# Layer two's second half: its second product in seven products too, and the leads set anew

## The chip, the cores and the metric

The kernel runs on one core of a Trainium2 chip. The core has five engines that each run their own instruction list: PE (TensorE, matmuls, with its weight loads listed as PEld), DVE (VectorE), ACT (ScalarE), POOL (GpSimd) and SP (SyncE), which here only issues DMAs. They meet through semaphores. The metric is the device time of one execution in microseconds.

## The reference

Attention of 8 heads over 4 x 576 positions (half of the heads see the last 32 positions, half every 32nd), then two feed-forward layers on 2304 tokens of 512 features, all in float32:

```python
# layer one (hidden size 1536): xn = x / rms(x) * rms_g
y = (silu(xn @ w_gate) * (xn @ w_val)) @ w_out
# layer two (hidden size 2048)
h = y @ w_in
out = (np.maximum(h, 0.0) ** 2) @ w_out
```

## The kernel before

**Precision.** Every factor of a product is split in two parts of float32r, hi = round(v) (ACT or DVE) and lo = v - hi (DVE or POOL). A product of a 128 x 128 block is then three matmuls: hi x hi, hi x lo, lo x hi. I call a factor that is split so a *form*.

**Stages.** Phase 0 is the first half of layer one and is interleaved with the attention. Phase 1 is the rest of layer one (three pairs of 128 hidden features, `j`), phases 2 and 3 are the two halves of layer two's hidden features (four pairs each). In phases 1 to 3 the tokens go in three pairs `q` of two tiles of 384 (`n` = 0, 1).

**The seven-product form.** The first product of each layer (x times `w_in`) in phases 1 to 3 is a 2 x 2 block product (two token tiles, two hidden blocks, two halves of the 512 features), done with seven block products instead of eight: sums and differences of the x blocks and of the weight blocks are made beforehand, and the seven results P1, P5, P6, P2, P7, P3, P4, in this order, are added up. `product` (L1785) issues six matmuls for each at L1806: two feature blocks of 128 x three. PSUM bank A takes P1; once it is copied out as s1, P6 and P7 and P4 are added on to A by PE. D takes P5 and then P3. C takes P2, which DVE adds to s1 (L1841). ReLU and square follow (L1857, L1905 to L1908), and the hidden tile is split (L1934 hi, L1941 lo).

**The second product**, hidden times `w_out`, is done plainly in all phases: `a_step` (L1955) takes one hidden tile of 128 features and one token tile and issues 4 output blocks x 3 matmuls (`mm3`, L1361 to L1363) into four banks that are accumulated over all `j`. In phase 3 the results of phase 2 (kept in `yq_d`) are added when the banks are read (L2010).

**x blocks.** For each `q` of phases 1 to 3, `pair_task` loads x (L1618), makes four differences (L1650) and seven forms (L1657, L1659 hi, L1664 lo) of 768 columns in `ra`. Phases 2 and 3 both do this, from the same data.

**Weights** come as raw float64 words (`wst_a<-in_w`), are converted on DVE and POOL, split, stored to DRAM (`wi_d` for the first product, `wo_d` for the second), and loaded again (L1344).

**What sets the order.** PE's order is a fixed list. All else (which engine takes an operation that two could do, and where in its list it stands) is decided while the kernel is built, by a planner that keeps a clock for each engine, takes the task that can start first, and breaks near ties by due times. Due times are positions in the stages less a lead (`W2_LEAD`, `X2_LEAD`, `PREP_LEAD` and others). Filler matmuls (`fill`, L2155) are put in where the planner sees PE waiting in the beginning.

Of the kernel before, what the change touches and what calls it, by code (L numbers as in the profile page):

```python
# [56 lines left out]
ATT_LEAD, ATT_STEP = 6.5, 0.25  # L57
PREP_LEAD = 4.192
W_LEAD = 0.5
X_LEAD = 2.784  # L60
# [4 lines left out]
TOL = 0.144  # L65
# [8 lines left out]
NM2 = 10  # L74
# [3 lines left out]
PRI = {"qk": -3, "mask": 4, "mx": 2, "exp": 1, "eps": 2, "sum": 8, "norm": -3, "turn": 1, "keep": 20, "tr": -1,  # L78
       "swap": -1, "pv": 3, "out": 0, "sq": -3, "ms0": 2, "add": 0}
MXP, LOADF, BIAS = 10, 0.5, 0.729  # L80

D_BUSY, D_COST, D_LATE, D_COST2 = 111.519, 1.1, 250.0, 0.5
PV_AHEAD = 4
# [20 lines left out]
NHID = len(HID_AT)  # L104
PRODUCTS = [
    ("P1", 0, 0, "A", None), ("P5", 3, 1, "D", None), ("P6", 4, 2, "A", "s1"), ("P2", 1, 3, "C", None),
    ("P7", 5, 4, "A", "u2"), ("P3", 6, 5, "D", "s5"), ("P4", 2, 6, "A", "c22"),
]
W2_LEAD, X2_LEAD, L2_LEAD = 3.0, 2.9, 3.0
X2_PRI = 1.0  # L110
# [90 lines left out]
def kernel(ctx: ExitStack, tc: tile.TileContext, loc, strd, w1, w2, g, cst, out):  # L201
# [73 lines left out]
    wo_d = {(ph, j): dram.tile([128, 2, 2, 512], F32R, name=f"wo_d{ph}{j}") for ph in NJS for j in range(NJS[ph])}  # L275
# [838 lines left out]

    def through(cell, t):
        cell["n"] += 1
        if cell["n"] == 2:
            cell["t"] = t

    def w_task(n, due):  # L1120
# [11 lines left out]
        def size(parts, t):  # L1132
            if not two:
                cell["w"], cell["ring"] = ring_take(n)
            if two:
                o = 1024 * is_out((ph2, j2, m2))
# [83 lines left out]
    def raw_ready(n):  # L1220
        k = n - U1
        return latest(done.get("raw"), *(done.get(("w2",) + u) for u in units2[:k] if not is_out(u) or is_out(units2[k])))

    def sums_ready(ph, j, m):
        k = units2.index((ph, j, m))
        return latest(0.0, *(done.get(("w2",) + u) for u in units2[:k] if is_out(u)))
# [34 lines left out]
    def pieces(ph, j, m):  # L1261

        outer = is_out((ph, j, m))

# [25 lines left out]
        def lo(a, b, o, c):  # L1290
            w = b - a

            def store(t):
                src = stage(c["n"])[:, 0:2 * w].bitcast(F32).rearrange("p (h c) -> p h c", h=2)
                if outer:
                    dst = wo_d[ph, j][:, o // 512]
                else:
                    dst = wi_d[ph, j, m][:, :, o:o + w]
                nc.sync.dma_start(out=dst.bitcast(F32), in_=src)
                end = lanes.dma(2 * w, t)  # L1300
                stage_t[c["n"]] = end
                if b == 2048:
                    done["stored", ph, j, m] = end

            def f(parts, t):
# [3 lines left out]
                if b == 2048:  # L1309
                    done["w2", ph, j, m] = t  # L1310
                spawn([Task(-2000, [(None, [[("Q", 0.0)]], lambda _, t: store(t), None)])], t)
# [3 lines left out]
        if not outer:  # L1315
# [281 lines left out]

    def pair_task(ph, q, due):
# [44 lines left out]
        def block(b, r, add, after):  # L1643
# [17 lines left out]
            def lo(parts, t):  # L1661
# [4 lines left out]
                done["xb", ph, q, b] = t  # L1666
                cell["n"] += 1
# [107 lines left out]
    def bank_take():  # L1775
        b = min((b for b in banks if bank_time(b) is not None), key=bank_time)
# [7 lines left out]

    def product(ph, q, j, m, p):  # L1785
        name, a, b, role, need = PRODUCTS[p]
        key = ph, q, j, m
# [36 lines left out]
    def after_product(key, name, c, at_t):  # L1824
# [12 lines left out]

        def add(what, role, h, n):
# [15 lines left out]
        def relu(h, n):  # L1854
            def f(_, t):
                e = f_take(ph)
                nc.scalar.activation(  # L1857
                    out=e["ap"](), in_=c["A"]["ap"][:, :SN], func=ACTF.Silu if ph == 1 else ACTF.Relu
                )
                c["A"]["t"] = t  # L1860
# [5 lines left out]
            if ph == 1 and m:  # L1866
                times_gate(None, h, n, at_t)
# [10 lines left out]
        def times_gate(e, h, n, at_t):  # L1878

            def f(_, t):  # L1880
                x = gates.pop((q, j, h, n))
                v = c["A"]["ap"][:, :SN] if e is None else e["ap"]()
                o = e or x
                nc.vector.tensor_tensor(out=o["ap"](), in0=v, in1=x["ap"](), op=ALU.mult)
                if e is None:
                    c["A"]["t"] = t
# [11 lines left out]
        def square(e, h, n, clipped, at_t):  # L1898
            seq = h_seq[ph, q, n, j, h]

            def f(parts, t):
# [7 lines left out]
                spawn([split(seq, e, -1000 + at[key] if n == 0 else -1000 + at[ph, q, "t"])], t)  # L1909
# [6 lines left out]
            "P1": lambda: copy("s1", "A"), "P5": lambda: copy("s5", "D"), "P6": lambda: copy("u2", "A"),  # L1916
            "P2": lambda: add("s1", "C", 0, 0), "P7": lambda: add("s5", "A", 1, 1), "P3": lambda: add("u2", "D", 0, 1),
            "P4": lambda: relu(1, 0),
# [11 lines left out]
    def split(seq, e, due):  # L1930
# [7 lines left out]
        def lo(parts, t):  # L1938
# [4 lines left out]
            e["t"] = t  # L1943

# [10 lines left out]
    def a_step(ph, q, n, j, h):  # L1955
# [7 lines left out]
        def f(ms):  # L1963
            def g(_, t):
                if first:
                    acc2[key] = [bank_take() for _ in range(KDM)]
                x, w = hid2(seq), w_out(j)[:, h]
# [10 lines left out]
        tail = ph == 3 and q == NQ - 1 and n == 1 and last  # L1978
        parts = [range(m, m + 1) for m in range(KDM)] if tail else [range(KDM)]
        return [(lambda: times() is not None, mms(SN, 3 * len(parts[0])), f(parts[0]), times)] + [  # L1980
            (None, mms(SN, 3), f(p), None) for p in parts[1:]
        ]
# [4 lines left out]
    def after_a(ph, q, n, ms, at_t):  # L1987
        cell = outs.setdefault((ph, q, n), {"n": 0, "t": 0.0, "ys": False})
        t0 = 2 * SN * q + SN * n
        dst = y1_d[:, :, t0:t0 + SN] if ph == 1 else (  # L1990
            yq_d[q][n] if ph == 2 else out[:, t0:t0 + SN].rearrange("(m p) t -> p m t", p=128)
        )
        tail = ph == 3 and q == NQ - 1 and n == 1
# [5 lines left out]

        def store_part(m):  # L2000
            return lambda t: nc.sync.dma_start(out=dst[:, m], in_=ys2[:, m])

        def evict(m):
            def f(parts, t):
# [4 lines left out]
                if ph != 2:  # L2009
# [8 lines left out]
                if tail:  # L2018
                    transfer(-2000, t, SN, store_part(m))
                if cell["n"] == KDM:  # L2020
                    if ph != 2:
                        done["yp2", ph, 2 * q + n] = cell["t"]
                    if not tail:
                        transfer(-2000, cell["t"], KDM * SN, store)
# [5 lines left out]
        def when():  # L2030
            return max(0.0 if cell["ys"] else rel["ys"][0], done["ypt", ph, q, n] if ph != 2 else 0.0)
# [4 lines left out]
    def yp2_task(ph, q, n, due):  # L2036
        nth = 2 * q + n

        def when():
            t0 = 2 * SN * q + SN * n  # L2040
            stored = [
                ("yp", i) for i, (o, m) in enumerate(BLOCKS) if o < t0 + SN and o + m > t0
            ] if ph == 1 else [("yq", 2, q, n)]
            if nth:
                before = [done.get(("yp2", ph, nth - 1))]
            elif ph == 1:
                before = [done.get("late")]
            else:
                before = [done.get(("in_used", 2, NJS[2] - 1))] + [f_time(e, 2) for e in f_tiles if e["last"] == 2]
            return latest(*before, *map(done.get, stored))  # L2050

        def load(_, t):
            if ph == 3 and nth == 0:
                for e in f_tiles:
                    if e["last"] == 2:
                        e["last"] = 0
            v = late["fb"][:, 0:KDM * SN].rearrange("p (k c) -> p k c", k=KDM)
            t0 = 2 * SN * q + SN * n
            nc.sync.dma_start(out=v, in_=yp_d[:, :, t0:t0 + SN] if ph == 1 else yq_d[q][n])
# [4 lines left out]

    slots = [(0, i, j) for i in range(NB) for j in range(PHASES[0][2])]
# [3 lines left out]
    starts = {1: ((0.0, 0.9), (1.8, 2.8), (4.1, 5.1)), 2: ((0.0,), (1.0,), (2.6,), (4.2,))}  # L2069
    for ph in NJS:  # L2070
        for q in range(NQ):
            for j, os in enumerate(starts[min(ph, 2)]):
                for m, o in enumerate(os):
                    at[ph, q, j, m] = n_at + o
            at[ph, q, "t"] = n_at + (6.3 if ph == 1 else 5.8)
            n_at += 8.3 if ph == 1 else 8.7
# [20 lines left out]
    for ph in NJS:  # L2097
        for q in range(NQ):
            pair_task(ph, q, at[ph, q, 0, 0] - X2_LEAD)
            for n in range(2):  # L2100
                if ph != 2:
# [3 lines left out]
    for ph, j, m in units2:  # L2105
# [3 lines left out]
        else:  # L2109
# [9 lines left out]
    for ph in NJS:  # L2119
        nj = NJS[ph]  # L2120
        for q in range(NQ):
            for j in range(nj):
                ps = [product(ph, q, j, m, p) for m in range(MATS[ph]) for p in range(len(PRODUCTS))]
                if j:
# [8 lines left out]
            for n, js in ((0, [nj - 1]), (1, range(nj))):  # L2133
# [6 lines left out]
    with tc.manual_schedule():  # L2140
# [45 lines left out]
        while tasks:  # L2186
            if "fb" not in late and order.get("prep", 0) == NB and all(
# [4 lines left out]
                late["fb"] = pool("fb", 1).tile([128, 6144], F32, name="fb")  # L2192
                late["rb"] = pool("rb", 1, reuse_waits="tile").tile([128, 2048 * NJS[1]], F32R, name="rb")
                late["fc"] = ExitStack()
                late["fd"] = pool("fd", 1, late["fc"]).tile([128, 2048], F32, name="fd")
            if not advance():
# [77 lines left out]
```

## Time and profile before

| | us |
|---|---|
| median of 3 runs (lowest, highest) | 906.1 (905.36, 907.96) |
| profiled execution, its own time | 904.4 |
| span of the profile, first to last instruction | 902.6 |
| mean granted clock of TensorE, share of full speed | 0.996 |

In the profile, a group row reads: line, engine, operation, output<-input, shapes, count, then busy us and the mean ns of one, then the idle time of the engine just ahead of these instructions and what ended it. Matmuls are pipelined: a row's length is that from a matmul's start to its modelled end, and the next starts before that end. The stages of the profile by time: phase 0 with the attention to about 298 us, phase 1 to about 512, phase 2 to about 712, phase 3 to the end.

### The profile page before, as it was taken

To read this page: it belongs to the slowest core of one execution; us is meant where nothing else is said; L and a number is where in the kernel's file an instruction comes from. 1 tells how busy PE (TensorE), PEld (TensorE's weight loads), DVE (VectorE), ACT (ScalarE), POOL (GpSimd) and SP (SyncE) were. 2 spreads that over 40 slices of the span, in tenths; PEclk is the share of its full clock that TensorE was granted. 3 is DMA by queue.
4 is the path that set the end of the run, shared out by engine and by line. 5 is a ranking of instruction groups with operands and counts; after the bars stand their busy time and mean duration, and the time that the engine had idled before them with its cause. 6 is when DMAs were issued, how large, how long until landed. Compare 5 with 4: busy or idle time off the path is not lost.

```text
span 902.6 us, 17050 instructions
## 1 busy us (share of the span) xinstructions
PE 884.5 (98%) x6809; PEld 827.7 (92%) x6814; DVE 652.8 (72%) x1071; ACT 441.8 (49%) x1107; POOL 80.3 (9%) x69
## 2 busy tenths in 40 slices
PE   8999999899999999999999999999999999999998
PEld 5778787788788999999999999999999999999998
DVE  5999967868868666967957968768869568346433
ACT  5978737332323454454444555457355445343441
POOL 0243400101000000200101101001000000000000
PEclk9999999999999999999999999999999999999999
DMA  9766643565675999999898796552673953302203
GB/s 342 248 234 202 204 146 96 201 228 168 210 291 186 373 380 348 371 390 363 312 355 320 282 343 232 177 193 103 229 266 142 380 202 104 107 1 71 71 1 105
DMA packets 74607, 202.50 MB, mean 224 GB/s; under 512 B 6432, under 2 KB 38176, under 8 KB 69792
## 3 DMA queue, kind: packets, MB, share of 16 engines
q1 hardware_dynamic: 74528, 201.42, 62.3%
q8 instruction: 53, 0.87, 0.4%
q14 instruction: 26, 0.21, 0.1%
HBM read 136.97 MB, written 60.82 MB: 219 GB/s over the span
## 4 chain that ended last, share of the span: by engine, by line
PE 84%; DVE 7%; DMA 6%; ACT 2%; issue 1%; SPq 0%; POOL 0%; DVEq 0%
PE a L1806 16%; PE pg L1806 8%; PE a L1361 7%; PE a L1362 7%; PE a L1363 7%; PE pb L1806 5%; DMA wst_a<-in_w 5%; PE gv L1361 5%; PE gv L1362 4%; PE gv L1363 4%; PE pg L1363 2%; PE pg L1361 2%; PE pg L1362 2%; PE pb L1363 2%; PE pb L1362 2%; PE pb L1361 2%
## 5 line engine op out<-in xcount | busy, mean ns | idle before, releaser
L1806 PE MATMUL a<-ra 128*128 128x384 f32 x990 | 189.0, 335 | 1.0 <-DVE fa L1841 1.0
L1806 PEld LDWEIGHTS a<-ra 128*128 128x128 f32 x990 | 173.7, 188 | 2.0 <-DVE fa L1841 1.9
L1806 PE MATMUL pg<-ra 128*128 128x384 f32 x492 | 95.7, 335 | 1.5 <-DVE fb L1841 1.4
L1361 PE MATMUL gv<-ra 128*128 128x512 f32 (+1 forms) x240 | 91.2, 380 | 0.4 <-DVE fa L1438 0.4
L1362 PE MATMUL gv<-ra 128*128 128x512 f32 (+1 forms) x240 | 88.9, 370 | 0.0
L1363 PE MATMUL gv<-ra 128*128 128x512 f32 (+1 forms) x240 | 88.7, 370 | 0.0
L1806 PEld LDWEIGHTS pg<-ra 128*128 128x128 f32 x492 | 86.3, 188 | 2.3 <-DVE fb L1841 1.7
L1363 PE MATMUL a<-ra,rb 128*128 128x384 f32 x216 | 72.6, 336 | 0.0
L1361 PE MATMUL a<-ra,rb 128*128 128x384 f32 x216 | 72.6, 336 | 0.0
L1362 PE MATMUL a<-ra,rb 128*128 128x384 f32 x216 | 72.6, 336 | 0.0
L1664 DVE TENSOR_TENSOR ra<-fb,ra 128x768 fp32r<-128x768 f32 x63 | 59.0, 953 | 1.6 <-ACT ra L1657 0.9
L1806 PE MATMUL pb<-ra 128*128 128x384 f32 x282 | 55.7, 336 | 0.3 <-DVE ra L1664 0.3
L1361 PEld LDWEIGHTS gv<-ra 128*128 128x128 f32 x240 | 45.5, 190 | 8.4 <-DVE fa L1438 0.6
L1363 PEld LDWEIGHTS gv<-ra 128*128 128x128 f32 x240 | 45.5, 190 | 7.8
L1362 PEld LDWEIGHTS gv<-ra 128*128 128x128 f32 x240 | 45.6, 190 | 7.3 <-DVE ra L934 0.3
L1806 PEld LDWEIGHTS pb<-ra 128*128 128x128 f32 x282 | 49.5, 188 | 0.8 <-DVE ra L1664 0.6
L1657 ACT ACTIVATE ra<-fb 128x768 fp32r<-128x768 f32 x47 | 39.3, 841 | 22.1 <-DVE fb L1650 12.9
L1308 DVE TENSOR_TENSOR wst_a<-fa,wst_a 128x512 fp32r<-128x512 f32 (+1 forms) x59 | 37.4, 638 | 15.8 <-ACT wst_a L1285 15.1
L1361 PE MATMUL a<-ra 128*128 128x512 f32 (+1 forms) x120 | 45.4, 379 | 2.3 <-ACT pt L545 1.5
L1285 ACT ACTIVATE wst_a<-fa 128x512 fp32r<-128x512 f32 (+1 forms) x60 | 34.3, 577 | 26.6 <-DMA wi_d<-wst_a 14.8
L1308 POOL TENSOR_TENSOR wst_a<-fa,wst_a 128x512 fp32r<-128x512 f32 (+1 forms) x19 | 26.3, 1383 | 221.3 <-ACT wst_a L1285 199.5
L1362 PE MATMUL a<-ra 128*128 128x512 f32 (+1 forms) x120 | 44.4, 370 | 0.1
(215 smaller groups left out, 1937.7 us busy)
## 6 DMA issues: line engine op xcount, KB each, us to landing
ra<-wi_d SPq DMA_DIRECT2D x26, 1792.0 KB, 8.2
wst_a<-in_w SPq DMA_DIRECT2D x34, 1024.0 KB, 6.6
wi_d<-wst_a SPq DMA_DIRECT2D x42, 512.0 KB, 4.9
wo_d<-wst_a SPq DMA_DIRECT2D x22, 512.0 KB, 10.2
rb<-wo_d SPq DMA_DIRECT2D x9, 1024.0 KB, 6.8
fb<-y_d SPq DMA_DIRECT2D x24, 384.0 KB, 4.9
fa<-in_strd SPq DMA_DIRECT2D x8, 604.0 KB, 5.9
fa<-in_loc SPq DMA_DIRECT2D x8, 592.0 KB, 5.3
```

What stands on the lines that cost most here:

```text
L1285: nc.scalar.activation(out=dst, in_=raw(a, b), func=ACTF.Copy)
L1308: eng.tensor_tensor(out=x[:, w:2 * w], in0=raw(a, b), in1=x[:, 0:w].bitcast(F32), op=ALU.subtract)
L1361: nc.tensor.matmul(out=o, lhsT=whi, rhs=x_hi, start=first, stop=False)
L1362: nc.tensor.matmul(out=o, lhsT=whi, rhs=x_lo, start=False, stop=False)
L1363: nc.tensor.matmul(out=o, lhsT=wlo, rhs=x_hi, start=False, stop=last)
L1657: nc.scalar.activation(out=x[:, 0], in_=src, func=ACTF.Copy)
L1664: eng.tensor_tensor(out=x[:, 1], in0=src, in1=x[:, 0].bitcast(F32), op=ALU.subtract)
L1806: nc.tensor.matmul(out=o, lhsT=l, rhs=v, start=need is None and k + n == 0, stop=k == 1 and n == 2, skip_group_check=need is not None,)
```

## The change

**The second product of phase 3** takes the seven-product form too. Its 2 x 2 blocks are the two token tiles, the two hidden blocks `h` of each pair `j`, and two halves of 256 output features. For each `q` there are seven products of four steps `j`, each step six matmuls (`o_step`, two output blocks x three). The hidden tiles stay as float32 until `hidden_form` makes the seven sums, differences and forms of each `j` from them, in up to twelve places (four in `ra`, eight new ones `rx`). The weight forms are made in `pieces` and stored in seven tensors `wf_d`; `o_load_task` brings them through four buffers (`ORING`). `after_o` adds each product's result to the output tile in `wst_a`, which starts as phase 2's result, and stores it.

**x forms of phase 3** are no longer made: phase 2 stores its seven forms per `q` to `xf_d` (`keep_form`), phase 3 loads them (`form_task`).

**The seed.** In phases 1 to 3, except for the first set, P1 is copied by ACT (DVE may take it too) into bank C (`seed`), and PE adds P2 onto it; ACT then reads the finished sum (`relu` with role C) where DVE had to add P2 to s1.

**Leads and costs** are set anew. They move instructions of the attention stage and of the weight preparation.

```diff
-W2_LEAD, X2_LEAD, L2_LEAD = 3.0, 2.9, 3.0
+W2_LEAD, X2_LEAD, L2_LEAD = 5.974, 3.127, 3.0
-    ("P1", 0, 0, "A", None), ("P5", 3, 1, "D", None), ("P6", 4, 2, "A", "s1"), ("P2", 1, 3, "C", None),
+    ("P1", 0, 0, "A", None), ("P5", 3, 1, "D", None), ("P6", 4, 2, "A", "s1"), ("P2", 1, 3, "C", "s1"),
+O_ORDER = [(0, 0), (0, 1), (1, 0), (1, 1), (0, 2), (1, 2), (0, 3), (1, 3)]
+O_ORDER += [(p, j) for p in range(2, 7) for j in range(4)]
...
+        def seed(what, role, to):
+            def f(parts, t):
+                c[to] = bank_take(True)
+                o, i = c[to]["ap"][:, :SN], c[role]["ap"][:, :SN]
+                if parts[0][0] == "A":
+                    nc.scalar.activation(out=o, in_=i, func=ACTF.Copy)
+                else:
+                    nc.vector.tensor_copy(o, i)
+                c[what] = t
...
-            "P1": lambda: copy("s1", "A"), "P5": lambda: copy("s5", "D"), "P6": lambda: copy("u2", "A"),
-            "P2": lambda: add("s1", "C", 0, 0), "P7": lambda: add("s5", "A", 1, 1), "P3": lambda: add("u2", "D", 0, 1),
+            "P1": lambda: seed("s1", "A", "C") if seeded(ph, q, j) else copy("s1", "A"), ...
+            "P2": lambda: relu("C", 0, 0) if seeded(ph, q, j) else add("s1", "C", 0, 0), ...
...
+        def load(_, t):
+            nc.sync.dma_start(out=x_slot2(b).bitcast(F32), in_=xf_d[q, b].bitcast(F32))
...
+    PARTS = [
+        ((0, 0), None, ()), ((0, 0), ((0, 1), (0, 0)), (("lo", 0),)), ((0, 0), ((1, 1), (0, 0)), (("lo", 1),)),
+        ((1, 0), None, ()), ((0, 1), ((1, 1), (0, 1)), (("sum", 1),)), ((1, 1), None, ()),
+        ((1, 0), ((1, 0), (0, 0)), (("lo", 3), ("sum", 2))),
+    ]
+    def hidden_form(q, j, p, seq, due):
...
+        def total(parts, t):
+            eng = nc.gpsimd if parts[0][0] == "P" else nc.vector
+            eng.tensor_tensor(out=tile_of(dst), in0=tile_of(add[0]), in1=tile_of(add[1]), op=ALU.subtract)
...
+        def lo(parts, t):
+            eng = nc.gpsimd if parts[0][0] == "P" else nc.vector
+            x = halves()
+            eng.tensor_tensor(out=x[:, 1], in0=tile_of(dst), in1=x[:, 0].bitcast(F32), op=ALU.subtract)
...
+    def o_load_task(q, p, due):
+        n = len(PRODUCTS) * q + p
+        a = PRODUCTS[p][1]
+        def when():
+            before = done.get(("out_used", 2, n)) if n < ORING else done.get(("o_used", n - ORING))
...
+    def o_step(q, p, j, ms=range(2)):
...
+            for m in ms:
+                w_hi, w_lo = (w[:, h, 128 * m:128 * m + 128] for h in range(2))
+                for i, (l, v) in enumerate(((w_hi, x[:, 0]), (w_hi, x[:, 1]), (w_lo, x[:, 0]))):
+                    nc.tensor.matmul(
+                        out=c[role, m]["ap"][:, :SN], lhsT=l, rhs=v, start=need is None and first and i == 0,
+                        stop=last and i == 2, skip_group_check=need is not None,
+                    )
...
+    def after_o(q, name, c, ms, at_t):
+        m0, n, role, what, end, frees = {
+            "P1": (0, 0, "A", "s1", False, False), "P5": (2, 1, "D", "s5", False, False),
+            "P6": (0, 1, "A", "u2", False, False), "P2": (0, 0, "C", None, True, True),
+            "P7": (2, 1, "A", "c22", True, False), "P3": (0, 1, "D", None, True, True),
+            "P4": (2, 0, "A", None, True, True),
+        }[name]
...
+                if ph == 3:
+                    row = ps
+                    if j == nj - 1:
+                        o = [o_step(q, p, i) for p, i in O_ORDER]
+                        if q == NQ - 1:
+                            o[-4:] = [o_step(q, 6, i, range(m, m + 1)) for m in range(2) for i in range(4)]
+                        row = ps[:3] + o[:2] + ps[3:5] + o[2:4] + ps[5:] + o[4:]
```

How this moves instructions, at three places. PE, the end of the program, before: the last output blocks of `a_step` for the last hidden tile (banks `a_...` and `pg_...`, hidden tile in `ra`, weights in `rc`).

```order
L1361 MATMUL a_3912<-ra,rc 128x384
L1362 MATMUL a_3912<-ra,rc 128x384
L1363 MATMUL a_3912<-ra,rc 128x384
L1361 MATMUL pg_3836<-ra,rc 128x384
L1362 MATMUL pg_3836<-ra,rc 128x384
L1363 MATMUL pg_3836<-ra,rc 128x384
```

The same place now: the last steps of P3 (forms in `rx_...`) and P4 (forms in `ra`); L2269 is `o_step`'s matmul.

```order
L2269 MATMUL a_3946<-rx_7151,rc 128x384 x3
L2269 MATMUL pg_3872<-rx_7152,rc 128x384 x3
L2269 MATMUL a_3946<-rx_7152,rc 128x384 x3
L2269 MATMUL pg_3917<-ra,rb 128x384 x12
L2269 MATMUL a_3945<-ra,rb 128x384 x12
```

Four banks that ran over all hidden tiles have become pairs of banks that run over the four `j` of one product.

ACT, the last set of first products in phase 3, before: L1832 copies P1, P5 and P6 out of PSUM, L1905 and L1906 are ReLU and square, L1934 is hi of a hidden form.

```order
L1832 ACTIVATE fa<-pg_3836 128x384
L1832 ACTIVATE fa<-a_3911 128x384
L1832 ACTIVATE wst_a<-pg_3836 128x384
L1905 ACTIVATE fa<-fa 128x384
L1906 ACTIVATE fa<-fa 128x384
L1934 ACTIVATE ra<-fa 128x384
```

The same place now: L1901 is the seed (PSUM bank to PSUM bank), L1890 copies P5 and P6 out, L1928 reads the finished sum from bank C, L1977 is the square, L2181 is hi of a hidden form.

```order
L1901 ACTIVATE pb_3836<-a_3945 128x384
L1890 ACTIVATE fa<-pg_3917 128x384
L1890 ACTIVATE wst_a<-a_3945 128x384
L1928 ACTIVATE fa<-pb_3836 128x384
L1977 ACTIVATE fa<-fa 128x384
L2181 ACTIVATE ra<-fa 128x384 x2
```

The copy of P1 now goes to a bank, and ACT reads the sum of P1 and P2 itself.

SP, phase 3 from its first output store on, before (`y_d` holds x, `yq_d` phase 2's result):

```order
L1996 DMA out<-fa 128x4x384
L2059 DMA fb<-yq_d_117 128x1536
L1618 DMA fb<-y_d 128x2x384 x4
L1996 DMA out<-fa 128x4x384
L2059 DMA fb<-yq_d_118 128x1536
```

And now, from the x forms of the second pair on: L1635 loads an x form, L2217 the weight form of one product into the ring, L2293 stores output.

```order
L1635 DMA ra<-xf_d_162 128x1536
L1635 DMA ra<-xf_d_163 128x1536
L2217 DMA rb<-wf_d_148 128x2048
L2217 DMA rb<-wf_d_149 128x2048
L2217 DMA rb<-wf_d_145 128x2048
L2217 DMA rc<-wf_d_143 128x2048
L2293 DMA out<-wst_a 128x384 x2
L2217 DMA rb<-wf_d_146 128x2048
```

The loads of the ring stand behind all x loads of the next pair, and output stores between them.

## Rows read from the trace of the kernel before

**Rows 1.** The page, part 1: busy us, share of the span, instructions.

```profile
PE 884.5 (98%) x6809; PEld 827.7 (92%) x6814; DVE 652.8 (72%) x1071; ACT 441.8 (49%) x1107; POOL 80.3 (9%) x69
```

**Rows 2.** By stage: us, busy of PE, PEld, DVE, ACT, POOL, clock, DMA share, GB/s.

```profile
0.00:298.00 298.00, 287.23 (x3354) 233.51 (x3360) 241.68 (x397) 159.26 (x573) 47.62 (x42) 0.99 0.64 215
298.00:512.00 214.00, 211.79 (x1245) 209.85 (x1244) 160.46 (x258) 101.05 (x187) 21.42 (x18) 1.00 0.92 347
512.00:712.00 200.00, 198.46 (x1140) 197.80 (x1139) 153.52 (x247) 102.60 (x194) 11.26 (x9) 1.00 0.63 225
712.00:898.00 186.00, 186.00 (x1072) 185.83 (x1071) 95.54 (x168) 78.87 (x153) 0.00 (x0) 1.00 0.28 98
```

**Rows 3.** Timeline of PE: start us, length us, line, operation.

```profile
8.99 3.88 PE L2155 MATMUL warm<-blank 128*128 128x512 bf16 x17 [0.16 <-issue]
...
58.79 0.61 PE L430 MATMUL sc<-cst_sb 128*128 128x384 f32 x2
...
876.33 0.34 PE L1363 MATMUL pg<-ra,rb 128*128 128x384 f32 x1
...
879.45 0.34 PE L1363 MATMUL pb<-ra,rc 128*128 128x384 f32 x1
```

**Rows 4.** PE's waits: us in total, times, longest.

```profile
PE xo L578 <- issue: 4.3, 2, 2.3
...
PE pg L1806 <- DVE fb L1841: 1.4, 1, 1.4
PE bc L886 <- DVE sm L456: 1.4, 1, 1.4
PE a L1806 <- DVE fa L1841: 1.0, 3, 0.4
...
PE pb L1806 <- DVE ra L1664: 0.3, 1, 0.3
PE pg L1806 <- ACT fb L1832: 0.2, 1, 0.2
```

**Rows 5.** DMA issues: count, KB each, median us to landing.

```profile
ra<-wi_d SPq DMA_DIRECT2D x26, 1792.0 KB, 8.2
...
rb<-wo_d SPq DMA_DIRECT2D x9, 1024.0 KB, 6.8
```

**Rows 6.** DVE's groups by shape, 712 to 898 us.

```profile
L1664 DVE TENSOR_TENSOR ra<-fb,ra 128x768 fp32r<-128x768 f32 x14 | 13.0, 954 | 0.5 <-ACT ra L1657 0.4
L1941 DVE TENSOR_TENSOR ra<-fa,ra 128x384 fp32r<-128x384 f32 x20 | 11.0, 554 | 4.0 <-ACT ra L1934 3.8
...
L1650 DVE TENSOR_TENSOR fb<-fb 128x768 f32<-128x768 f32 x8 | 7.6, 953 | 0.1
...
L1941 DVE TENSOR_TENSOR ra<-wst_a,ra 128x384 fp32r<-128x384 f32 x13 | 7.0, 555 | 5.9 <-ACT ra L1934 5.9
```

**Rows 7.** ACT's groups by shape, 712 to 898 us.

```profile
L1657 ACT ACTIVATE ra<-fb 128x768 fp32r<-128x768 f32 x8 | 6.7, 838 | 1.1 <-PE a L1806 0.6 <-PE pg L1806 0.6
...
L1832 ACT ACTIVATE fa<-a 128x384 f32<-128x384 f32 x10 | 4.9, 492 | 5.4 <-PE a L1806 5.3
```

**Rows 8.** Timeline of DVE at two places.

```profile
346.49 0.56 DVE L1884 TENSOR_TENSOR fa<-pg,fa 128x384 f32<-128x384 f32 x1
...
347.90 0.55 DVE L1941 TENSOR_TENSOR ra<-fa,ra 128x384 fp32r<-128x384 f32 x1
...
684.63 1.83 DVE L1664 TENSOR_TENSOR ra<-fb,ra 128x768 fp32r<-128x768 f32 x2
```

**Rows 9.** Timeline of POOL and DVE at two places.

```profile
433.44 1.33 POOL L1308 TENSOR_TENSOR wst_a<-fa,wst_a 128x512 fp32r<-128x512 f32 x1 [2.64 <-issue]
433.51 1.67 DVE L1884 TENSOR_TENSOR fd<-fd 128x384 f32<-128x384 f32 x1
...
495.63 0.91 POOL L1271 TENSOR_TENSOR fa<-fa 128x256 f32<-128x256 f32 x1 [11.15 <-DVE fa L1165]
```

**Rows 10.** Timeline of DVE, its last instruction.

```profile
899.07 0.56 DVE L2010 TENSOR_TENSOR fa<-pg,fb 128x384 f32<-128x384 f32 x1
```

More of the change, by code (lines that the diff above doesn't have):

```diff
@@ L64 @@
 DRAIN = 0.12
-TOL = 0.144
+TOL = 0.141
 FILL, FILL_OF, T0, W1_AT = 0.215, 0.85, 5.3, 11.631
@@ L1263, in pieces @@
         outer = is_out((ph, j, m))
+        forms = outer and ph == 3
         def raw(a, b):
@@ L1976, in f @@
             return g
[L1978 to L1982, printed above, removed]
+        return [(lambda: times() is not None, mms(SN, 3 * KDM), f(range(KDM)), times)]
     ys2 = qa[:, YS2:YS2 + KDM * SN].rearrange("p (k c) -> p k c", k=KDM)
@@ L1989, in after_a @@
         t0 = 2 * SN * q + SN * n
[L1990 to L1993, printed above, removed]
+        dst = y1_d[:, :, t0:t0 + SN] if ph == 1 else yq_d[q][n]
         def store(t):
@@ new lines, in o_slot, with when, load @@
+    def o_slot(n):
+        n %= ORING
+        a = late["rc"] if n == NJS[1] else late["rb"][:, 2048 * n:2048 * n + 2048]
+        return a.rearrange("p (j h c) -> p j h c", j=NJS[3], h=2)
+    def o_load_task(q, p, due):
+        n = len(PRODUCTS) * q + p
+        a = PRODUCTS[p][1]
+        def when():
+            before = done.get(("out_used", 2, n)) if n < ORING else done.get(("o_used", n - ORING))
+            return latest(before, *(done.get(("stored", 3, j, MATS[3])) for j in range(NJS[3])))
+        def load(_, t):
+            nc.sync.dma_start(out=o_slot(n).bitcast(F32), in_=wf_d[a].bitcast(F32))
+            done["o_in", n] = lanes.dma(2048, t)
+        tasks.append(Task(due, [(lambda: when() is not None, [[("Q", 0.0)]], load, when)]))
@@ new lines, with y_tile, y_load_task, when @@
+    y3 = {}
+    def y_tile(m, n):
+        o = SN * (KDM * n + m)
+        return wst_a[:, o:o + SN].bitcast(F32)
+    def y_load_task(q, n, due):
+        def when():
+            before = [done.get(("out", q - 1, m, n)) for m in range(KDM)] if q else [made_all()]
+            return latest(done.get(("yq", 2, q, n)), *before)
+        def load(_, t):
+            o = SN * KDM * n
+            nc.sync.dma_start(
+                out=wst_a[:, o:o + KDM * SN].bitcast(F32).rearrange("p (k c) -> p k c", k=KDM), in_=yq_d[q][n]
+            )
+            done["y", q, n] = lanes.dma(KDM * SN, t)
+        tasks.append(Task(due, [(lambda: when() is not None, [[("Q", 0.0)]], load, when)]))
@@ L2108 @@
                 load2_task(ph, j, m, at[ph, q, j, m] - L2_LEAD, MATS[1] * (NJS[1] * q + j) + m)
-        else:
+        elif not (ph == 3 and is_out((ph, j, m))):
             load2_task(ph, j, m, at[ph, 0, j, 0] + is_out((ph, j, m)) - L2_LEAD)
@@ L2195 @@
                 late["fd"] = pool("fd", 1, late["fc"]).tile([128, 2048], F32, name="fd")
+            if "rx" not in late and "split2" in done and ("xs2", 2 * NQ - 1) in done:
+                late["fs"].close()
+                rx = pool("rx", 1, side="right", reuse_waits="tile")
+                late["rx"] = [rx.tile([128, 2 * SN], F32R, tag=f"x{k}", name=f"rx{k}") for k in range(8)]
             if not advance():
```

303 lines of the change are left out of this document (230 added, 73 removed).

## The prediction

> **What bounds the kernel now.** First the busy times: PE is busy 98% of the span, DVE 72%, ACT 49% [rows 1]. By stage (attention with the first half of layer one to 298 us, the rest of layer one to about 512, layer two's first half to about 712, its second half to the end) PE misses 10.8, 2.2, 1.5 and 0.0 us of its stretch [rows 2]. So after 298 us nearly every microsecond is a matmul, and only fewer matmuls, or waits that come new, can move the time there. In the last stage DVE is busy 95.5 of 186 us, ACT 78.9, POOL not at all, and the DMA engines carry 98 GB/s against 347 in the stage from 298 on [rows 2]: room for what the change adds. The table of waits names the few that PE has; after 298 us they are four lines on L1806, 2.9 us in all [rows 4]. Last the rate: eighteen 128x384 matmuls start between 876.33 and 879.45, 0.1733 us apart [rows 3]. A row's "0.34 us" is the pipelined length, not the price.
>
> **The change, part by part.**
>
> *Matmuls.* Before, the second product of the second half takes 2 token halves x 4 j x 2 hidden halves x 4 output blocks x 3 = 192 matmuls per pair of token tiles; after, 7 products x 4 j x 2 blocks x 3 = 168. Three pairs: 72 fewer, x 0.1733 = 12.5 us, all on the path, since PE never waits in that stage. The first product keeps its 168. The Trainium skill's page "TensorE: Matmul & The Clock Gate", section "Back-to-back issue gap", would price a warm matmul at N/2.4 + 2.5 ns, 162.5 ns here, and the saving at 11.7 us. The rows say 0.1733, and I go by them; nothing else hangs on that sentence.
>
> *The x forms of the second half.* They are no longer made anew: 21 of 768 columns are stored in the first half and loaded again. This takes 22 DVE subtractions of 0.953 us out of the last stage [rows 6] and, before it, those of its first pair. One wait goes with them: PE's longest after 298 us, 1.4 us on DVE L1841 [rows 4], stands behind two such subtractions at 684.63 [rows 8]. From there to the last stage's first product (898.9 - 1080 x 0.1733 = 711.7) no other wait is in the table, so nothing shown is late next: -1.4.
>
> *Forms of the hidden tile.* DVE and POOL now make 84 hidden forms instead of 48, and 48 differences ahead of them; 42 additions replace 24. DVE's own last stage: 95.5 - 21.0 (x forms) - 6.7 (12 additions of the second product P2) - 13.3 (24 evictions) + 23.3 (42 additions) + 21.6 (39 differences) + 10.0 (18 more forms), each of the 384-column ones at 0.555 [rows 6], = 109 us. The order puts 27 of these operations on POOL. A POOL operation of 512 columns took 1.33 us at 433.44; a DVE subtraction of two SBUF operands that began 0.07 later took 1.67 instead of 0.55 and ended 0.41 after POOL [rows 9]. So POOL holds DVE; it adds little. At about 1.0 us each (between 0.91 for 256 columns and 1.33 for 512 [rows 9]), 27 us of holding. 136 of 173.5 us: room on average. The Trainium skill says the same in "GPSIMD Engine Reference", section "1. Specifications": POOL shares its SBUF interfaces with VectorE, with contention where DVE reads two SBUF inputs. The rows agree; it speaks against this change, and is weighed in the third rival.
>
> In the seven second products that end a pair, the tail, PE runs 24 steps of 6 matmuls, 25.0 us. DVE has 20 forms, 12 differences and 14 additions, 46 operations that start 0.47 us apart when back to back (four from 346.49 to 347.90, [rows 8]), 21.6 us. Close, but up to 12 forms lie finished ahead. Bounds: nothing, or 6 us a tail (third rival). I take 0.3 us a tail, the size of the short waits of before [rows 4]: +0.9.
>
> *The seed.* P2 now adds onto a copy of P1 in another bank. The copy is ACT's in all 40 cases by the order; before, DVE shared this work. An ACT copy from PSUM to SBUF took 0.492 us [rows 7]; none from PSUM to PSUM is in the trace: between 0.49 and, if ACT stands behind an x form of 0.838 [rows 7], 1.3 us. Behind it on ACT stand the copies of P5 and P6; P6 waits for it first, and P5's six matmuls, 1.04 us, cover it. Before, that wait cost 0.2 us in all (pg <- ACT fb L1832, [rows 4]). Nothing at the lower bound; at the upper 0.3 x 40 = 12 us. I take +0.6, the row being the nearer. P2's result then needs no addition on DVE (0.555), only ACT's.
>
> *Data.* Second-half weights of the second product now come through a ring of four buffers, 21 loads of 1 MB, with 16.5 MB of x forms: some 48 MB in 173.5 us, 277 GB/s, less than the 347 that left PE only 2.2 us idle in layer one [rows 2]. The tightest load is P7's: its buffer is P1's, free with P1's last step; until P7 begins PE has 54 matmuls, 9.4 us. Such a load landed in 6.8 us [rows 5]. On SP it is queued behind seven x loads, each waiting for PE's last use of its block; the last of these is free 3.1 us earlier. Free, unless a landing passes 9.4. The first half gains 16.5 MB of stores in 187 us, 88 GB/s on 225: also below 347. 0.
>
> *Start and end.* The new leads put eight more filler matmuls into PE's order before 50 us (0.228 each [rows 3]) and one fewer pair of mask matmuls (0.61). Fillers stand where PE would wait: 0 to +1.8; half is 0.9, less 0.6: +0.3. Otherwise the 10.8 us of stage one are dealt anew, and I can't read how: 0, with -5 to +4 as bounds (half of them gone, or a third more). The end remains as it is: from 899.07 one DVE addition of 0.56 and a store [rows 10].
>
> Sum on the profiled execution: 904.4 (902.6 span, 1.8 around it) - 12.5 - 1.4 + 0.9 + 0.6 + 0.3 = 892.3. That execution lies 1.7 below the median of the runs, 0.96 below the fastest; I add 1.0: **893.3 us**. About 0.3%, 2.7 us, is what a measurement can tell from no change.
>
> **Rivals.**
>
> 1. *The new leads win as well.* Half of stage one's 10.8 us of waits go: 893.3 - 5 = 888. For: weights are begun earlier, and the largest waits of the stage are single stalls of 1.4 to 2.3 us [rows 4]. Against: two of them are "issue" before bursts of small matmuls, which stay. 14%.
>
> 2. *The seeds and first additions give part back.* 40 seeds late by 0.2 us: +8, less the 0.6 counted: 901. For: one engine makes them all. Against: ACT is busy under half the time in each stage after 298 [rows 2]. 15%.
>
> 3. *The tails become DVE's: slower.* In the trace each form's DVE half waits 0.2 to 0.45 us for ACT's half (4.0 over 20, 5.9 over 13, [rows 6]); at 0.30 more for 20 forms and 0.555 for 26 others a tail costs 31.5 us against PE's 25.0, and 9 POOL operations of a pair that hold DVE add up to 0.41 each [rows 9], 3.7 us. 10.2 x 3 = 31 us late, less what the forms made ahead cover (between nothing and 12 x 0.855 us a tail): 0 to +31, middle 909 or more. It decides from (908.8 - 893.3) / 3 = 5.2 us a tail on. Against: ACT runs ahead where forms stand in a row, DVE then starts every 0.47 [rows 8]. 5%.
>
> 4. *No change: the ring is late.* P7's load lands in 13 us instead of 6.8, and P3's and P4's after it: 3.6 us a pair, 10.8 in all, 904. For: 8.2 us for 1.8 MB under load [rows 5], SP's order is strict. Against: 48 MB is under what was carried before. 5%.
>
> The forecast, 889.5 to 897 by its own bounds, has 61%. Range 888 to 900: below and above it stay about 2 in 10 (part of 1, part of 2, rivals 3 and 4). Faster by over 0.3% (under 903.4): 61 + 14 + 15 = 90%; within: 5%; slower: 5%.
>
> **What would show it.** Right: 66 fewer matmuls in PE's count (72 less, 8 fillers more, 2 masks less), the last stage some 12.5 us shorter with PE busy throughout, DVE there at about 63%, DMA near 277 GB/s; no PE wait on DVE L1841's successor behind an x subtraction near the start of the last stage. Wrong: PE waits "<- ACT" at the seed's or P6's line of over 3 us in all (rival 2); in the three tails waits on DVE's form line (rival 3) or on a DMA into the weight ring (rival 4); a first product of the last stage that starts more than 3 us earlier or later than 711 (stage one dealt anew).

## The result and the profile after

The changed kernel took 893.58 us (median of 4 runs, 890.77 to 894.51) against 907.03 for the kernel before on the same chip: ratio 0.9847, interval 0.9823 to 0.9872. 893.3 was forecast. The profiled execution took 894.51, its span 892.7 (before: 904.4 and 902.6).

PE's share is as before [rows 1]; the busy times of the page:

```profile
PE 872.9 (98%) x6748; PEld 814.3 (91%) x6748; DVE 648.3 (73%) x1083; ACT 452.2 (51%) x1148; POOL 112.1 (13%) x101
```

By stage (start:end, length, then busy us and instructions of PE, PEld, DVE, ACT, POOL, granted clock, DMA share, GB/s), to be laid beside [rows 2]:

```profile
0.00:298.00 298.00, 288.22 (x3380) 233.91 (x3381) 239.94 (x400) 159.97 (x572) 50.53 (x45) 0.99 0.65 218
298.00:510.00 212.00, 207.88 (x1218) 205.99 (x1217) 151.09 (x246) 95.63 (x178) 17.01 (x17) 1.00 0.94 353
510.00:714.50 204.50, 202.70 (x1164) 201.75 (x1163) 149.84 (x248) 109.19 (x215) 13.94 (x13) 1.00 0.89 328
714.50:888.00 173.50, 172.97 (x988) 171.84 (x987) 106.89 (x190) 87.40 (x184) 30.59 (x27) 1.00 0.70 256
```

The last stage, from its first product to the last matmul's end, has gone from 188.0 us (711.03 to 899.03) to 177.5 (711.67 to 889.16). PE's timelines, before and then after:

```profile
711.03 3.30 PE L1806 MATMUL a<-ra 128*128 128x384 f32 x18
...
898.69 0.34 PE L1363 MATMUL pg<-ra,rc 128*128 128x384 f32 x1
```

```profile
711.67 1.22 PE L1864 MATMUL a<-ra 128*128 128x384 f32 x6
...
886.91 2.25 PE L2269 MATMUL a<-ra,rb 128*128 128x384 f32 x12
```

DVE is busy 62% of it, DMA carries 256 GB/s (63% and 277 were said). PE misses 4.1 us from 298 to 510, nearly twice the 2.2 of before. The waits after 298 us (line, what ended the wait, sum, count, longest), to be read against [rows 4]:

```profile
PE a L1864 <- DVE fa L1912: 3.0, 3, 1.3
PE pg L1864 <- ACT a L1901: 1.4, 1, 1.4
PE pg L1864 <- ACT fd L1890: 1.2, 1, 1.2
```

The 1.4 us behind an x form are gone; seeds and copies (L1901, L1890) have brought 2.6, the addition of P7 (L1912) 3.0. (Before, PE also waited 0.9 us for ACT at 313.58, which the prediction's 2.9 us after 298 leaves out.) One of the three waits on L1912, in DVE's and PE's timelines:

```profile
492.36 1.23 DVE L1176 SCALAR_TENSOR_TENSOR fa<-wst_a,fa 128x1024 int32<-128x1024 int32 x1
493.50 0.55 DVE L1912 TENSOR_TENSOR fa<-a,fa 128x384 f32<-128x384 f32 x1
...
494.11 3.22 PE L1864 MATMUL a<-ra 128*128 128x384 f32 x17 [1.14 <-DVE fa L1912]
```

DVE is converting weights (L1176) when P7 ends, and PE's P4 waits for the addition that stands behind it. So the time was right, and the shares within it were not. The experiments show by how much.

### The profile page after: what moved, and what is told of

The parts are those of the page before. It is cut to its first block, busy times and chain, and to the rows that moved or that the text cites. A ratio compares the mean times of both kernels' runs of the same rounds, so it can differ in the third digit from the quotient of the medians.

```text
span 892.7 us, 17232 instructions
## 1 busy us (share of the span) xinstructions
PE 872.9 (98%) x6748; PEld 814.3 (91%) x6748; DVE 648.3 (73%) x1083; ACT 452.2 (51%) x1148; POOL 112.1 (13%) x101
## 5 line engine op out<-in xcount | busy, mean ns | idle before, releaser
L1864 PE MATMUL a<-ra 128*128 128x384 f32 x864 | 166.3, 336 | 3.2 <-DVE fa L1912 3.0
L1864 PEld LDWEIGHTS a<-ra 128*128 128x128 f32 x864 | 151.5, 188 | 4.8 <-DVE fa L1912 3.9
L1864 PE MATMUL pb<-ra 128*128 128x384 f32 x414 | 82.8, 335 | 0.1
L1864 PEld LDWEIGHTS pb<-ra 128*128 128x128 f32 x414 | 72.8, 188 | 0.8 <-DVE fb L1912 0.5
L1326 DVE TENSOR_TENSOR wst_a<-fa,wst_a 128x512 fp32r<-128x512 f32 (+1 forms) x65 | 41.0, 631 | 25.7 <-ACT wst_a L1299 24.8
L1299 ACT ACTIVATE wst_a<-fa 128x512 fp32r<-128x512 f32 (+1 forms) x58 | 33.0, 569 | 37.9 <-DMA wi_d<-wst_a 21.3
L1388 PE MATMUL a<-ra,rb 128*128 128x384 f32 x144 | 48.5, 337 | 0.0
L1389 PE MATMUL a<-ra,rb 128*128 128x384 f32 x144 | 48.4, 336 | 0.0
L1387 PE MATMUL a<-ra,rb 128*128 128x384 f32 x144 | 48.4, 336 | 0.0
L1387 PE MATMUL a<-ra 128*128 128x512 f32 (+1 forms) x120 | 45.0, 375 | 0.0
L1388 PE MATMUL a<-ra 128*128 128x512 f32 (+1 forms) x120 | 44.3, 369 | 0.7 <-DVE ra L1486 0.7
L1389 PE MATMUL a<-ra 128*128 128x512 f32 (+1 forms) x120 | 44.2, 368 | 0.0
L1171 DVE SCALAR_TENSOR_TENSOR fa<-wst_a,fa 128x1024 int32<-128x1024 int32 x34 | 42.5, 1250 | 0.8
```

What stands on the lines that cost most here:

```text
L1171: nc.vector.scalar_tensor_tensor(out=bits(), in0=word(1), scalar=-0x40000000, in1=bits(), op0=ALU.bitwise_and, op1=ALU.bitwise_or)
L1299: nc.scalar.activation(out=dst, in_=raw(a, b), func=ACTF.Copy)
L1326: eng.tensor_tensor(out=x[:, w:2 * w], in0=raw(a, b), in1=x[:, 0:w].bitcast(F32), op=ALU.subtract)
L1387: nc.tensor.matmul(out=o, lhsT=whi, rhs=x_hi, start=first, stop=False)
L1388: nc.tensor.matmul(out=o, lhsT=whi, rhs=x_lo, start=False, stop=False)
L1389: nc.tensor.matmul(out=o, lhsT=wlo, rhs=x_hi, start=False, stop=last)
```

## The experiments

Each is compared with the kernel before on the same chip. Because the granted clock in the first 60 us differs between executions (below), the table also gives, from PE's timeline of each profiled execution, the start of phase 1's first product, the time from there to the last stage's first product (phases 1 and 2), and the length of the last stage; then PE's waits from the start of phase 1 on, their sum and the longest.

| | median | ratio, interval | start | phases 1, 2 | last stage | waits, longest |
|---|---|---|---|---|---|---|
| before | 907.0 | 1 | 309.4 | 401.6 | 188.0 | 3.7, 1.4 |
| changed | 893.6 | 0.985, 0.982 to 0.987 | 307.7 | 404.0 | 177.5 | 6.3, 1.4 |
| again | 895.4 | 0.987, 0.985 to 0.990 | 307.2 | 402.3 | 176.8 | 4.2, 1.1 |
| no_seed | 908.4 | 1.002, 1.001 to 1.003 | 307.8 | 404.2 | 193.2 | 16.1, 6.1 |
| old_leads | 907.7 | 1.001, 0.999 to 1.002 | 311.9 | 415.1 | 176.0 | 14.2, 6.8 |
| o_only | 917.7 | 1.012, 1.010 to 1.015 | 312.1 | 416.6 | 187.5 | 20.1, 6.5 |
| seed_12 | 893.0 | 0.984, 0.981 to 0.987 | 306.9 | 405.0 | 177.3 | 6.4, 2.1 |
| seed_3 | 911.3 | 1.004, 1.002 to 1.006 | 308.9 | 406.2 | 191.9 | 19.4, 12.4 |
| one_lead | 902.9 | 0.995, 0.993 to 0.997 | 306.4 | 411.3 | 176.7 | 11.3, 5.8 |
| before_ls | 912.1 | 1.005, 1.003 to 1.007 | 307.4 | 408.9 | 187.9 | 9.5, 3.6 |
| ns_light | 903.2 | 0.994, 0.992 to 0.997 | 314.0 | 407.1 | 178.3 | 8.9, 1.6 |
| twice | 919.0 | 1.014, 1.011 to 1.015 | 310.7 | 400.4 | 201.9 | 21.2, 1.7 |
| no_pool | 892.9 | 0.984, 0.982 to 0.986 | 307.5 | 402.9 | 177.7 | 5.0, 1.5 |
| ring_3 | 901.3 | 0.993, 0.991 to 0.995 | 310.9 | 404.4 | 180.8 | 8.7, 2.5 |

Two columns carry the argument. With the new second product the last stage takes 176 to 178 us where the seeds of phases 1 and 2 stand, or where the weights are less work (ns_light); twice and ring_3, which load that stage itself, are longer. Without these seeds it takes 187 to 193, as long as with the plain second product (188) or longer. Phases 1 and 2 take 9 to 14 us longer than in "again" where the old `X2_PRI` stands with the new second product (one_lead, old_leads, o_only). "changed" and "again" are the same kernel and differ by 1.7 and 0.7 us in these columns, so differences of 2 us say little.

**again**: the changed kernel beside the first four.

> The changed kernel once more, beside the others on this chip. All theories: within 0.3% of 893.6 us, and in its trace the same two kinds of PE waits after 298 us: on the addition of P7 (DVE L1912, 3 us in all) and on ACT's seeds and copies (L1901, L1890, 2 to 3 us).

As expected in time. The same waits stand there, shorter: 1.8 and 0.4 us on L1912, 1.6 on L1890 and L1901.

**no_seed**

```diff
     def seeded(ph, q, j):
-        return (ph, q, j) != (1, 0, 0)
+        return False
```

> Without the seed: P1 is copied to SBUF and DVE adds P2 to it, as in the kernel before; all else as changed. DVE gets 40 additions of 0.556 us from PSUM (22 us), ACT loses some copies of 0.475 us. Theory of the prediction (the seed costs little, +0.6): within 2 us of the changed kernel, PE's waits from 298 us to the last stage between 3 and 8 us. Rival A (the seed gives back some of the gain, 2.6 us of waits on ACT in the trace): 2 to 4 us faster, and these waits gone. Rival B (the seed pays by emptying DVE ahead of P7's addition): 3 us slower or more, waits on L1912 twice as long as the 3.3 us seen.

13 us slower: all of the gain is gone, and of the three cases only B has the sign right, with the wrong place. Waits on L1912 grew little (4.2 us from phase 1 on, against 3.3 in the changed kernel and 2.3 in "again"). The loss is in the last stage, 193.2 us against 176.8 in "again": PE, then ACT, in their timelines, then PE's stretch (columns as above):

```profile
729.73 1.21 PE L1864 MATMUL pg<-ra 128*128 128x384 f32 x6
737.07 6.07 PE L1864 MATMUL a<-ra 128*128 128x384 f32 x18 [6.14 <-ACT fa L1890]
...
736.01 0.63 ACT L1299 ACTIVATE wst_a<-fa 128x512 fp32r<-128x512 f32 x1 [2.30 <-DMA wf_d<-wst_a]
736.55 0.47 ACT L1890 ACTIVATE fa<-a 128x384 f32<-128x384 f32 x1
```

```profile
730.00:740.00 10.00, 3.86 (x15) 3.54 (x14) 4.78 (x9) 3.73 (x9) 0.00 (x0) 0.81 0.54 183
```

ACT does not copy P1's result before 736.55, because ahead of the copy it rounds weight forms (L1299) into a staging buffer that is being stored. The weights of the last stage are late, and an in-order engine passes this on to PE. After the stall 18 matmuls take 6.07 us, where 18 at 726.61 took 3.28. The granted clock is 0.81 over these 10 us: part of the matmuls ran at 1.2 GHz instead of 2.4. Two more waits follow, of 2.4 and 1.8 us.

**old_leads**

```diff
-ATT_LEAD, ATT_STEP = 5.322, 0.059
+ATT_LEAD, ATT_STEP = 6.5, 0.25
...
-X2_PRI = 2.025
+X2_PRI = 1.0
```

> The changed kernel with the leads and costs of the kernel before (the leads of the new steps stay). PE gets 8 filler matmuls fewer and 2 mask matmuls more. Theory of the prediction (stage one is dealt anew without a net gain): within 3 us of the changed kernel, PE's waits in the first 300 us 10 to 12 us against 9.8. Rival (the leads win time too): 4 us slower or more, and that in the first 300 us. Second rival (they lose time in the stages after 298 us, where PE now waits 5.9 us instead of 3.8): 2 us faster or more, the waits there under 4 us.

12 us slower, the rival's sign, but not its place: of the 16.7 us between the profiled executions of this kernel and "again", 4.7 lie before phase 1 and 12.8 in phases 1 and 2; the last stage is 0.8 shorter. PE and SP in this kernel, then SP in "again":

```profile
362.64 0.32 SPq L1370 DMA_DIRECT2D rb<-wo_d  x1
...
373.00 0.66 PE L1387 MATMUL a<-ra,rb 128*128 128x384 f32 x1 [6.77 <-DMA rb<-wo_d]
```

```profile
353.49 0.32 SPq L1370 DMA_DIRECT2D rb<-wo_d  x1
```

The third weight block of layer one's second product is asked for 9 us later, lands after 10.4 us (DMA carries 414 GB/s from 360 to 370), and PE is there first.

**o_only**: both edits.

> Old leads and no seed: what is left of the change is the second product of the last stage in seven products and its stored x forms. Theory of the prediction (all of the gain is the 72 matmuls fewer): within 2 us of the changed kernel, so 12 to 15 us below the kernel before, the last stage 174.7 us of matmuls with under 2 us of waits. Rival (leads and seed carry part of the gain): 4 us or more above the changed kernel.

My theory fell by 22 us: alone, the second product and the stored x forms make the kernel 11 us *slower* than before, although 72 matmuls are gone. Its last stage is as long as before (187.5 us), and phases 1 and 2 are 15.0 us longer.

```profile
PE a L1387 <- DMA rb<-wo_d: 6.5, 1, 6.5
PE pg L2269 <- DMA rb<-wf_d: 3.5, 2, 2.4
PE pg L1864 <- DMA ra<-wi_d: 3.0, 1, 3.0
```

Three kinds of weight load are late. The next four kernels take that apart.

**seed_12** and **seed_3**

```diff
-        return (ph, q, j) != (1, 0, 0)
+        return (ph, q, j) != (1, 0, 0) and ph < 3     # seed_12
+        return ph == 3                                # seed_3
```

> Seeds in phases 1 and 2 only (28 of 40); in the last stage DVE adds P2 as before the change. Without any seed the time was 908.4 us against 895.4, and PE stood 6.1 us at 731, in the last stage's first pair, behind an ACT copy that stood in ACT's list behind the last rounding of second-product weights; these were stored until 738 us, against 715 with the seeds. Theory W (the seeds pay by freeing DVE in phases 1 and 2, where it prepares those weights; in the last stage they hardly matter): within 3 us of the changed kernel, 893 to 898, last weight store near 716. Rival L (the last stage's own DVE work needs them): 900 or more, waits on DVE after 715 us.

> The reverse: seeds in the last stage only (12 of 40). DVE has 28 additions of 0.556 us more, 15.6 us, while it prepares weights. Theory W: 902 to 910, with the last store of weight forms at 725 us or later and a PE stall of 3 us or more in the last stage's first pair, behind which the granted clock falls. Rival L: under 898, no such stall.

Theory W in both (seed_3 at 911.3 lies 1.3 us above its range). 28 seeds before the last stage do all that 40 do; of the 12 within it no effect shows. In seed_3 the last weight store and the first load of the ring, and PE behind it:

```profile
727.12 11.32 SPq L1311 DMA_DIRECT2D wf_d<-wst_a  x7
743.03 1.50 SPq L2217 DMA_DIRECT2D rb<-wf_d  x3
...
753.96 1.33 PE L2269 MATMUL a<-rx,rb 128*128 128x384 f32 x3 [12.41 <-DMA rb<-wf_d]
```

In the changed kernel that store comes at 718.13 and that load at 720.46, 17 us before PE's first `o_step`.

**one_lead**

```diff
-X2_PRI = 2.025
+X2_PRI = 1.0
```

> The changed kernel with one number of before: X2_PRI 1.0 instead of 2.025 (how early x blocks are due). With all the old leads the time was 907.7, with a wait of 6.8 us at 366 on the load of the second product's third weight block, which was issued at 362.6 against 353.5, and the clock at half speed behind it. Theory F (one late load and the clock that falls behind it make most of what the old leads cost): such a wait of 4 us or more at 366, and 900 to 906 us. Rival S (the loss is spread over the order as a whole): under 898, no single wait over 3 us after 300 us.

Theory F: 902.9, with one wait of 5.8 us at the foretold place. The load is issued at 356.70; nine matmuls behind the wait start about 0.32 us apart, then 0.173 again:

```profile
366.37 0.66 PE L1387 MATMUL a<-ra,rb 128*128 128x384 f32 x1 [5.84 <-DMA rb<-wo_d]
366.82 0.52 PE L1388 MATMUL a<-ra,rb 128*128 128x384 f32 x1
```

These nine take 3.00 us instead of 1.56: the slow clock behind this stall costs 1.4 us beside the 5.8. Against old_leads, phases 1 and 2 are 3.8 us shorter; 2.9 of it are PE's waits, 14.2 there and 11.3 here, so the rest of what the old leads cost there is mostly more of the short waits.

**before_ls**: the kernel before with the new constants and with `seed`, `whole_time` and the new `relu` put in.

> The kernel before with the new leads and with the seed, without the new second product and without stored x forms: both halves of layer two do the second product plainly and make their x forms. Theory of the prediction (matmuls are the gain, the rest is even): within 3 us of the kernel before; then the second product is worth 11 to 14 us where leads and seed stand with it, though alone it cost 11. Rival G (leads and seed gain 10 us or more for any kernel, since they did so in the changed one): 897 or less.

5 us slower than before, so neither theory has the size; G is out. The two largest waits are again a weight load and a DVE addition:

```profile
PE a L1361 <- DMA rb<-wo_d: 3.6, 1, 3.6
PE a L1815 <- DVE fb L1863: 3.3, 1, 3.3
```

Both lie before the last stage: phases 1 and 2 are 7.3 us longer than before, the last stage is as before. Without the second product leads and seed lose 5 us; without them it loses 11; together they gain 13. The last stage of the changed kernel is 10.4 us shorter than here, 11.1 in "again": with leads and seed in both, this is what the second product and its stored x forms are worth there. The stored forms were not run alone, and neither were the leads or the seed.

**ns_light**: as no_seed, and

```diff
+        NC = 64 if ph2 == 3 else 512
-            c = cell["r"]
+            c = cell["r"][:, :, :NC]
```

(the same in the three `bits` steps and their costs).

> No seed anywhere, but the weights of the last stage (both products, 8 blocks) are converted from float64 only in 64 of every 512 columns, and the planner knows it: four DVE instructions a block, 3.84 us, become some 0.7 us, about 25 us of DVE less between 510 and 730 us. This leaves the other columns unconverted. Theory W (the seed paid only by giving DVE time for these weights): the 13 us come back without it, 893 to 899, last store of weight forms before 722 us, no PE wait over 3 us after 700. Rival P (the additions of P2 on DVE hold up PE by themselves): 904 or more.

The kernel leaves out the conversion of 448 of every 512 columns of these weights. Its median lies between the two, but the last stage decides between them: 178.3 us, so 14.9 of the 16.4 us by which no_seed's exceeds that of "again" are back, and no wait after 700 us is over 1.6. (The last weight store still comes at 725.8 us, later than W said.) Phases 1 and 2 are 4.8 us longer than in "again", with short waits, most of them behind DVE's additions (L1913) and ACT's copies (L1891):

```profile
PE a L1865 <- DVE fa L1913: 2.9, 5, 1.3
PE a L1865 <- ACT fa L1891: 2.1, 2, 1.6
PE pg L1865 <- ACT fb L1891: 1.5, 1, 1.5
```

The additions alone do not show this price: no_seed makes the same ones and is only 1.9 us longer than "again" there, and from 548 us on the planner puts ns_light's work in another order. So W carries nearly all that the seeds give, about 15 us, and about 2 us at most are left for rival P. The median is raised further by the start: phase 1 began at 314.0 in the profiled execution.

**twice**

```diff
-            eng.tensor_tensor(out=x[:, 1], ...)
+            for _ in range(2):
+                eng.tensor_tensor(out=x[:, 1], ...)
```

> The changed kernel with the low half of each of the 84 hidden forms computed twice, in the same order: 66 subtractions of 0.555 us more on DVE (37 us on 107 of 173.5 us in the last stage) and 18 of 1.1 us more on POOL. In the tail from 800 to 826 us DVE was busy 20.8 of 26 us; 20 forms make that 31. Theory of the third rival, hard form (the tail's DVE work decides as soon as it exceeds PE's 25 us): about 6 us late in each of three tails, 908 to 914, with PE waits behind the form line L2188. Theory of the prediction (up to 12 forms ahead cover 10 us a tail): under 899.

The hard form, and worse. Waits in the three tails, then the last stage:

```profile
PE pg L2270 <- DVE rx L2189: 6.9, 7, 1.3
PE pg L2270 <- issue: 3.7, 4, 1.7
PE a L2270 <- DVE ra L2189: 2.9, 3, 1.2
```

```profile
714.50:915.00 200.50, 180.16 (x990) 169.68 (x988) 153.41 (x257) 87.33 (x184) 52.65 (x45) 1.00 0.60 221
```

18.3 us in 21 waits, 6.1 a tail. The last stage is 24.2 longer than no_pool's, which has no wait there. A matmul is shown 0.34 long while the next starts after 0.17, so each wait costs 0.17 more than its row; and behind the first matmul after a wait the next starts 0.25 to 0.29 us later instead of 0.17, some 0.1 more: 18.3 + 21 x 0.27 = 24.0. The granted clock stays at 1.00 through these short waits.

**no_pool**

```diff
-            (lambda: inputs() is not None, [dvx(SN), gps(SN)], total, inputs)
+            (lambda: inputs() is not None, [dvx(SN)], total, inputs)
```

(the same for `lo`.)

> Differences and low halves of the hidden forms on DVE alone: DVE takes the 27 operations that POOL did in the last stage (15.0 us at 0.555; POOL took 30.6 us for them). In the changed kernel DVE's low halves took 0.636 to 0.878 us and its squares 0.727 against 0.553 alone, some 10 us of holding in all. Theory of the prediction (POOL adds little, since it holds DVE): within 3 us of the changed kernel, these means back at 0.55. Rival (POOL carries what DVE could not do in the tails): 4 us slower or more, PE waits behind L2188.

As predicted. DVE in the last stage, without POOL:

```profile
L2188 DVE TENSOR_TENSOR rx<-fa,rx 128x384 fp32r<-128x384 f32 x51 | 26.5, 551 | 1.6 <-ACT rx L2181 1.2
L1979 DVE SCALAR_TENSOR_TENSOR fa<-fa 128x384 f32<-128x384 f32 x15 | 8.3, 555 | 0.2
```

```profile
714.50:888.00 173.50, 173.50 (x986) 171.08 (x984) 110.77 (x220) 85.90 (x180) 0.00 (x0) 1.00 0.70 254
```

DVE does 30 operations more, POOL's 27 and 3 of ACT's, in 3.9 us more (110.8 against 106.9). In the changed kernel POOL takes 30.6 us to save these 3.9. The rule of the Trainium skill ("GPSIMD Engine Reference", section "1. Specifications": contention where DVE reads two SBUF inputs) agrees: three such operations took 1.37 us each from 814.94 on, while POOL was at work, against 0.55 here.

**ring_3**

```diff
-ORING = 4
+ORING = 3
```

> Three buffers for the second product's weights in the last stage instead of four. A load can then start only when the product three places before is done, so two products, 2 x 4.17 us = 8.3 us, cover it, where three, 12.5 us, did. Loads rb<-wf_d took 8.1 us in the median. Theory D (the landing decides): short waits of 0 to 3 us on a DMA at some of the four late products of each pair, 4 to 12 us in all, 898 to 906. Rival (the loads stay covered, as the prediction had it with four): within 2 us of the changed kernel.

Theory D by the total, but only in part by the cause. The last stage's waits:

```profile
PE pg L2269 <- DMA rb<-wf_d: 1.9, 1, 1.9
PE pg L2269 <- ACT ra L2181: 1.6, 1, 1.6
```

One load is late, by 1.9 us. The last stage is 3.1 us longer than no_pool's, and these two waits account for it. Another 1.5 us lie in phases 1 and 2 and 3.4 before them, where the two kernels have the same instructions in the same order (up to 717 us on every engine), the granted clock in ring_3 being 0.74 from 40 to 50 us. Whether that is chance in all six runs is open, and so is any price of the third buffer beyond about 3 us.

## Why the prediction was right in its number and wrong in its shares

- *Matmuls, -12.5.* PEld counts 6814 before and 6748 now: the 66 fewer. The stage is shorter by 10.5. One wait takes 0.53 + 0.27; the new steps start a little further apart than [rows 3]: 120 from 804.96 to 825.93, 0.1748 us each, which is 0.7 us on 504. 0.5 stays unexplained. In "again", one_lead and old_leads, with the same matmuls and no wait in that stage, it is 11.2, 11.3 and 12.0 shorter than before. Mechanism right, size 0.5 to 2 us off.
- *x forms, -1.4.* The wait is gone. Others came in phases 1 and 2, which are 2.3 us longer than before (0.7 in "again").
- *Hidden forms, tails: +0.9.* 0.53 us in one wait, at 718.62 behind an addition of P7 and so ahead of the tails; none in a tail. The reason I gave, that forms made ahead cover, failed: in "twice" each tail was late by about the excess of DVE's work. The tail holds because 20.8 us of DVE fit into 26. The holding, put at 27 us, is about 10.
- *Seed, +0.6.* This is the step that failed: "P2's result then needs no addition on DVE" stood in it without a price. An ACT copy from PSUM to PSUM took 0.475 us (0.49 taken), the waits on ACT 2.6 us. But in phases 1 and 2 DVE prepares the last stage's weights, busy 75 to 77% [rows 2]; 28 additions there push the last store from 718 to 738 us, too late for PE, and the last stage takes 192 to 193 us instead of 177. So the seeds save about 15 us where the sum had a cost of 0.6.
- *Data, 0.* Three late loads show that its price is zero only while each is issued early enough; in o_only they cost 13 us of waits. Four buffers did suffice.
- *Start and leads, +0.3.* Phase 1 began 1.7 us earlier. "The 10.8 us of stage one are dealt anew" missed what the leads do after 298 us: they keep one load in time, worth 7 to 8 of their 12 us (one_lead); most of the rest are short waits in phases 1 and 2 (old_leads), which I have not traced one by one.

The profiled executions differ by 9.9 us, 2.2 less than my sum (12.1); that of "again" by 12.7, the medians by 13.4. So the sum lies within the spread of the executions, and that the forecast met the median to 0.3 us is luck. The forecast took the leads and the seed as right without asking what the second product would cost without them: a sum of each edit's own price, made on a schedule that had no late load because those edits kept it free. That this gave the right total is no proof of its shares.

## What to carry to other kernels

Work put on an engine that is not the bound, or taken off it, leaves the time alone only if nothing with a due time is queued there: look up what fills its gaps (here weight preparation), when the last of it must be stored, and by how many us it makes that. When several edits come together, price each with the others taken away too. And where an engine's in-order list holds a wait on a DMA, everything behind it inherits that wait.

## What the runs showed of the hardware

- ACT copies 128x384 float32 from PSUM to PSUM in 0.475 us, all 40 between 0.474 and 0.477; to SBUF 0.492.

```profile
L1901 ACT ACTIVATE pg<-a x9: 475/475/477, 459.6 to 846.5; 128x384 f32<-128x384 f32 x9
```

- Single stalls of about 6 us were followed by matmuls at 1.2 GHz, 0.32 us apart: nine after 5.84 us (one_lead), about 18 after 6.14 (no_seed). 21 waits of under 1.8 us left the granted clock at 1.00 (twice). Between these lengths it went either way: in seed_12 eleven matmuls started about 0.32 us apart after 2.06 us (granted clock 0.50 from 354 to 357 us); in before_ls none did after 3.31 us (1.00 from 692 to 695):

```profile
353.65 2.21 PE L1864 MATMUL a<-ra 128*128 128x384 f32 x6 [2.06 <-DVE fa L1912]
```

```profile
692.26 1.32 PE L1815 MATMUL a<-ra 128*128 128x384 f32 x6 [3.31 <-DVE fb L1863]
```

- In the first 60 us the granted clock differs between executions of the same instructions: 1.00 from 40 to 60 us in no_pool, 0.83 in ns_light, whose lists are the same up to 326 us on every engine, and phase 1 began at 307.5 and 314.0.
